# Attention probabilities transposed by VectorE and a trip through DRAM instead of by TensorE

## The chip, the cores and the metric

The kernel runs on one core of one Trainium2 chip. A time is the device time of one execution in microseconds (us), shorter being better. A comparison of two kernels is made between executions on the same chip.

## The reference

Pooled attention, and behind it a gated feed-forward block, in 32-bit floats:

```python
# q, k, v: [8 batches, 8 heads, 576, 64]
k_p = k.reshape(B, H, 72, 8, D).mean(axis=3)          # 576 keys pooled to 72
v_p = v.reshape(B, H, 72, 8, D).mean(axis=3)
scores = (1 / 8) * q @ k_p^T                           # [B, H, 576, 72]
attn = softmax(scores)                                 # 1e-9 added to the sum
x = (attn @ v_p) as [4608 tokens, 512]
out = ((x @ w1) * (x @ w2)) @ w3 @ w_out               # d_ff 1024, out [4608, 512]
```

## The kernel before

The 4608 tokens are worked in 12 chunks of 384. A chunk lies either in one batch (three tiles of 128 tokens) or across two (four tiles of 96): chunks 1, 4, 7 and 10 have four tiles, the others three. At the start w3 and w_out are multiplied into one matrix W, so that a chunk's feed-forward part is, for each of 8 blocks j of the inner dimension, a product a (12 matmuls, `a_mm`), a product b (12 matmuls, `b_mm`), their elementwise product g, and 9 matmuls of g with W (`out_mm`). The precision of a 32-bit product is kept by splitting each operand into a rounded high part and the remainder (hi and lo, or h and l in names) and doing three or four passes.

All work is written in one order by hand. A plan gives every piece of work a step; the pieces are sorted by step and, within a step, by kind: L (loads and stores on the DMA queue of SyncE, called SP), P (work of VectorE, ScalarE and GpSimd), M (feed-forward matmuls), A (attention matmuls). Each engine then runs its own pieces strictly in that order. A chunk m of the feed-forward part takes 24 steps: block j has its a at step 3j, its b at 3j+1 and its `out_mm` at 3j+5. The attention of chunk n stands in the same 24 steps as the feed-forward part of chunk n-1, which is called a period here. The attention of chunk 0 stands in the start, and that of chunk 1 in the period of chunk 0, where the weights w1 and w2 are still being split as well.

Attention of a chunk, for each token tile t: `s_mm` (scores, 8 matmuls in two halves), `soft1` and `soft2` (the softmax, in the tile E, 8 heads by 72 keys), `soft3` (the remainder keys copied to R), `pt_mm` and `ptr_mm` (transposes on TensorE into PSUM), `pt_post` and `ptr_post` (from PSUM into PTh, PTl and PTr). The 72 keys of a head are 64 main keys and 8 remainder keys. For a pair of heads 128 main keys make one 128-row transposed tile, four such for 8 heads; the 8x8 remainder keys, twice for the precision split, make two more. So a token tile has six transposes. When all tiles are through, `av_mm` (for each of four head pairs: PTh and PTl by the pooled values vbd, PTr by the remainder values VR) makes x for the chunk, and `av_post` splits it into the two tiles xT.

Other names: `qs` is the staging tile of q with one buffer, `qT` is q transposed by VectorE (`tr_q`), `st` the staging tiles of k and v with four buffers, POOL is GpSimd. The pool of PSUM for attention (`att`) has three buffers. `prep_vr` and `prep_vr2` pool and place the remainder values in VR.

The steps of the plan that matter, k being the first step of the period:

```python
s0, pt, av = (3, 5.5, 20.5) if n == 1 else (0, 6, 17) if nt == 4 else (0, 5, 15)
s_at = [k + s0 + 3 * t for t in range(nt)]
plan_att(n, s_at, 1, [x + pt for x in s_at], [k + av + pr for pr in range(NPR)])
plan_q(n, k - 18, 1, k - 9, 1)      # loads of q from step k-18, tr_q from step k-9
```

Of the kernel before, what the change touches and what calls it, by code (L numbers as in the profile page):

```python
# [18 lines left out]
def kernel(  # L19
# [52 lines left out]
    msk = cp.tile([P, 2], F32, name="msk")  # L72
# [182 lines left out]

    def load_q(n, prs=range(NPR)):
        if ("q", n) not in stage:
            stage["q", n] = p1.tile([P, NPR, CH // 32, 32], F32, tag="qs", name="qs")
        t = stage["q", n]
        for pr in prs:  # L260
            for (b, s0, cnt, off) in pieces(n):
                for par in range(2):
                    for db in range(2):
                        g = 2 * par + db
                        nc.sync.dma_start(
                            out=t[32 * g:32 * g + 32, pr, off // 32:(off + cnt) // 32],
                            in_=q[b, 2 * pr + par, s0:s0 + cnt, 32 * db:32 * db + 32].rearrange(
                                "(n t) e -> t n e", t=32),
                        )
# [3 lines left out]
    def tr_q(n, pr):  # L273
        if pr == 0:
            qT[n] = p1.tile([P, NPR, CH], F32, tag="qT", name="qT")
        nc.vector.transpose(
            out=qT[n][:, pr], in_=stage["q", n][:, pr].rearrange("p n e -> p (n e)"))
# [140 lines left out]

    def soft3(n, t):
        b, off, nt = tok_tiles(n)[t]  # L420
        E = Et[n, t]
        R = Rt[n, t] = p2.tile([P, NPR, 2, 2, 2, KR], F32R, tag="R", name="R")
        er = E[:nt].rearrange("p (a h) (x e) -> p a (h x) e", h=2, e=KR)[:, :, 0:18:17, :]
        for dup in range(2):
            nc.scalar.copy(out=R[:nt, :, :, dup, 0], in_=er)
        for dup in range(2):
            nc.vector.tensor_tensor(
                out=R[:nt, :, :, dup, 1], in0=er, in1=f(R[:nt, :, :, dup, 0]), op=ALU.subtract)
# [38 lines left out]
    def av_mm(n, pr):  # L467
        ps = patt.tile([P, 512], F32, tag="att", name="att")
        for (b, s0, cnt, off) in pieces(n):
# [3 lines left out]
            nc.tensor.matmul(out=o, lhsT=vh, rhs=PTh[n][:, pr, c], start=True, stop=False)  # L473
            nc.tensor.matmul(out=o, lhsT=vh, rhs=PTl[n][:, pr, c], start=False, stop=False)  # L474
            nc.tensor.matmul(out=o, lhsT=vl, rhs=PTh[n][:, pr, c], start=False, stop=False)  # L475
            nc.tensor.matmul(out=o, lhsT=VR[b % 2][:, pr], rhs=PTr[n][:, pr // 2, c], start=False, stop=True)  # L476
# [245 lines left out]
```

## Time and profile before

| What | us |
|---|---|
| median of 3 runs (lowest, highest) | 811.12 (809.81, 812.19) |
| span of the profiled execution, first to last instruction | 808.3 |
| PE (TensorE matmuls) busy | 776.7 |
| PEld (TensorE weight loads) busy | 722.8 |
| DVE (VectorE) busy | 431.2 |
| ACT (ScalarE) busy | 283.5 |
| POOL (GpSimd) busy | 193.8 |

The profile is of one execution, whose span is 2.8 us below the median of the runs. A row of the profile names the engine, the line of the kernel, the operation, what it wrote and read, and how often; then the busy time and the mean of one in nanoseconds, or in a timeline the start and the length. Matmuls are pipelined: one begins before the one ahead has ended, so what a matmul costs is the distance from its start to the start of the next, not its length. The granted TensorE clock was 0.985 of full speed on average.

### The profile page before, as it was taken

Reading aid. Unit: us, or ns where it says so; the run is one execution under the profiler, and the core shown is the slowest. Engines: PE = TensorE matmul, PEld = TensorE weight load, DVE = VectorE, ACT = ScalarE, POOL = GpSimd, SP = SyncE. Lnnn points to the kernel's source line nnn. Section 1 sums busy time; section 2 is a strip of 40 time slices with the busy share of each in tenths; the row PEclk is TensorE's granted clock in tenths of the full one; section 3 lists DMA queues with packets and bytes.
Section 4 is the critical chain, followed back from the end, with each engine's and each line's share of the span. In section 5 each row is a group of like instructions: output and inputs, shape, how many; then the busy total and the mean of one; then the engine's idle time right before and its main releaser. Section 6 shows DMA issues by size and latency. Waiting matters only on the chain.

```text
span 808.3 us, 11614 instructions
## 1 busy us (share of the span) xinstructions
PE 776.7 (96%) x4320; PEld 722.8 (89%) x4320; DVE 431.2 (53%) x881; ACT 283.5 (35%) x719; POOL 193.8 (24%) x234
## 2 busy tenths in 40 slices
PE   8879688899999999999999999999999999999998
PEld 7668677799999999999999999999999999999997
DVE  7858789556364465365374374374464465452112
ACT  5556555333233233242243233232233333232211
POOL 2244464207005403016008202034018021000000
PEclk9989899999999999999999999999999999999999
DMA  9997882036024230053034030071043110100101
GB/s 325 258 203 177 254 176 41 0 70 146 1 62 91 65 79 1 1 117 99 1 81 115 20 80 1 1 165 51 29 91 97 49 31 1 40 1 1 40 0 40
DMA packets 113160, 62.63 MB, mean 77 GB/s; under 512 B 80208, under 2 KB 96848, under 8 KB 113104
## 3 DMA queue, kind: packets, MB, share of 16 engines
q1 hardware_dynamic: 113104, 61.89, 30.7%
q8 instruction: 34, 0.56, 0.3%
q14 instruction: 22, 0.18, 0.1%
HBM read 52.43 MB, written 9.44 MB: 77 GB/s over the span
## 4 chain that ended last, share of the span: by engine, by line
PE 86%; DMA 5%; DVE 4%; issue 1%; SPq 1%; ACT 1%; POOL 0%; DVEq 0%
PE a L499 24%; PE b L499 24%; PE o L534 24%; PE att L378 4%; DMA st<-in_k_dram 2%; PE o L560 2%; PE att L438 2%; PE att L475 1%; PE att L473 1%; PE att L474 1%; PE att L476 1%; DMA qs<-in_q_dram 1%; PE att L448 1%; DVE wb L148 1%; DMA raw<-in_moe_w_out_dram 1%
## 5 line engine op out<-in xcount | busy, mean ns | idle before, releaser
L499 PE MATMUL a<-xT,hl 128*128 128x384 f32 x1152 | 222.6, 342 | 0.0
L499 PE MATMUL b<-xT,hl 128*128 128x384 f32 x1152 | 220.2, 339 | 0.0
L499 PEld LDWEIGHTS a<-xT,hl 128*128 128x128 f32 x1152 | 205.1, 191 | 4.7
L499 PEld LDWEIGHTS b<-xT,hl 128*128 128x128 f32 x1152 | 198.7, 188 | 0.0
L534 PE MATMUL o<-Wc,gh 128*128 128x512 f32 x576 | 183.6, 400 | 0.0
L534 PEld LDWEIGHTS o<-Wc,gh 128*128 128x128 f32 x576 | 105.2, 189 | 17.3
L519 DVE TENSOR_TENSOR a<-b,a 128x384 f32<-128x384 f32 x96 | 53.1, 554 | 125.6 <-PE b L499 125.6
L336 POOL TENSOR_TENSOR st<-st 72x512 f32<-72x512 f32 (+1 forms) x53 | 71.8, 1354 | 178.2 <-DMA st<-in_k_dram 163.5
L534 PE MATMUL o<-Wc,gl 128*128 128x512 f32 x288 | 114.0, 396 | 0.0
L509 ACT COPY a<-a 128x384 f32<-128x384 f32 x96 | 46.0, 479 | 182.3 <-PE a L499 163.3
L520 ACT CAST gh<-a 128x384 fp32r<-128x384 f32 x96 | 49.2, 512 | 147.8 <-DVE a L519 147.8
L525 DVE TENSOR_TENSOR gl<-a,gh 128x384 fp32r<-128x384 f32 x96 | 63.2, 659 | 35.8 <-ACT gh L520 35.4
L349 POOL TENSOR_TENSOR vbd<-vm,vbd 64x256 fp32r<-64x256 f32 x16 | 13.5, 842 | 253.3 <-ACT vbd L348 250.1
L534 PEld LDWEIGHTS o<-Wc,gl 128*128 128x128 f32 x288 | 54.1, 188 | 12.5
L485 DVE TENSOR_TENSOR xT<-att,xT 128x384 fp32r<-128x384 f32 x48 | 26.6, 556 | 70.7 <-ACT xT L484 70.7
L378 PE MATMUL att<-kbd,qT 128*128 128x144 f32 (+1 forms) x320 | 52.9, 289 | 4.3 <-ACT E L404 4.3
L400 DVE TENSOR_REDUCE sm<-E 128x4 f32<-128x288 f32 (+1 forms) x70 | 31.6, 451 | 46.3 <-ACT E L399 46.3
L378 PEld LDWEIGHTS att<-kbd,qT 128*128 128x128 f32 (+1 forms) x320 | 46.9, 180 | 5.7 <-ACT E L404 4.8
L394 DVE TENSOR_REDUCE mx<-att 128x4 f32<-128x288 f32 (+1 forms) x80 | 35.9, 450 | 28.1 <-PE att L378 28.1
L399 ACT ACTIVATE E<-E 128x288 f32<-128x288 f32 (+1 forms) x70 | 31.2, 445 | 55.5 <-DVE E L396 55.5
L560 PE MATMUL o<-hl 128*128 128x512 f32 x144 | 40.7, 421 | 4.8 <-DVE hl L177 4.8
L337 POOL TENSOR_TENSOR st<-st 72x256 f32<-72x256 f32 (+1 forms) x53 | 41.6, 784 | 4.2
(84 smaller groups left out, 796.0 us busy)
## 6 DMA issues: line engine op xcount, KB each, us to landing
raw<-in_moe_w_dram SPq DMA_DIRECT2D x32, 512.0 KB
st<-in_k_dram SPq DMA_DIRECT2D x32, 288.0 KB
out_dram<-ob SPq DMA_DIRECT2D x35, 256.0 KB
st<-in_v_dram SPq DMA_DIRECT2D x32, 256.0 KB
qs<-in_q_dram SPq DMA_DIRECT2D x128, 48.0 KB
raw<-in_moe_w_out_dram SPq DMA_DIRECT2D x8, 512.0 KB
st<-in_v_dram SPq DMA_DIRECT2D x64, 64.0 KB
qs<-in_q_dram SPq DMA_DIRECT2D x128, 24.0 KB
```

The source lines that it names most:

```text
L336: nc.gpsimd.tensor_tensor(out=t[:, :, 0:4], in0=t[:, :, 0:4], in1=t[:, :, 4:8], op=ALU.add)
L337: nc.gpsimd.tensor_tensor(out=t[:, :, 0:2], in0=t[:, :, 0:2], in1=t[:, :, 2:4], op=ALU.add)
L378: nc.tensor.matmul(out=ps[:nt, 2 * KP * j:2 * KP * (j + 1)], lhsT=qT[n][:, pr, off:off + nt], rhs=kbd[b % 2][:, pr], start=True, stop=True,)
L394: nc.vector.tensor_reduce(out=mx[:nt, hs], in_=sv, axis=AX.X, op=ALU.min)
L400: nc.vector.reduce_sum(out=sm[:nt, hs], in_=E[:nt, hs], axis=AX.X)
L499: nc.tensor.matmul(out=o, lhsT=w12[j, w][sw][:, kt * P:(kt + 1) * P], rhs=x[sx][:, kt], start=(i == 0), stop=(i == 3 * NK - 1))
L509: nc.scalar.copy(out=a, in_=gt[m, j][:, :CH])
L519: nc.vector.tensor_tensor(out=g, in0=ps[:, :CH], in1=g, op=ALU.mult)
L520: nc.scalar.copy(out=gh, in_=g)
L525: nc.vector.tensor_tensor(out=gl, in0=g, in1=f(gh), op=ALU.subtract)
L534: nc.tensor.matmul(out=oacc[m][t], lhsT=(gh, gl)[sg][:, c], rhs=W[j][sw], start=(j == 0 and i == 0), stop=(j == NJ - 1 and i == 2))
L560: nc.tensor.matmul(out=wacc[h][it], lhsT=w3t[s][sa][:, it * P:(it + 1) * P], rhs=wo[j][sb], start=(j == 0 and i == 0), stop=(j == NJ - 1 a ...
```

## The change

For chunks 1 to 11 (`n >= NT`, NT = 1) the six TensorE transposes of a token tile go, and with them `soft3`, `pt_post` and `ptr_post`. Instead:

- `te_turn`: VectorE transposes 32x32 blocks of E in place of the main keys into a tile T (which shares its buffer with `qs`), and of the remainder keys into Tr (which shares its buffers with R).
- `te_out`: two stores write T and Tr to a DRAM tile D. A chunk of three tiles has one such stage, a chunk of four tiles two, each of two tiles.
- `te_in`: eight loads bring D back with the blocks moved to their partitions: four into PTl (32 partitions each), four into PTr, which is the same data four times over.
- `te_post`, `te_rest`: ScalarE rounds PTl into PTh and the upper half of PTr, VectorE subtracts to leave the remainders, now once for half a chunk (128x768) and not once for a tile.
- The tokens of a chunk stand in another order within it (`tr_q` writes q in that order).
- In all chunks the remainder rows are re-laid: `load_vr` loads 8 rows of each head once and not four times, `prep_vr` copies them on chip, `prep_vr2` masks 128 rows and no longer adds 32.
- The steps move: scores come 2.5 steps apart and not 3 in chunks of four tiles, `av_mm` starts at step 19 (four tiles), 16 (three tiles) and not at 17 and 15, q is loaded from step k-8 and turned from k-4.

```diff
+    def te_turn(n, t):
+        ...
+        main = E[:nt].rearrange("p (a h) k -> p a (h k)", h=2)[:, :, KR:KR + P]
+        nc.vector.transpose(out=T[:nt, i, :, :, x].rearrange("p k a e -> p a k e"), in_=main)
+        nc.vector.transpose(out=Tr[:nt, i, :, x], in_=rest_keys(E, nt))
+
+    def te_out(n, i):
+        ...
+        d = stage["D", n, i] = dp.tile([P, 18 * 96], F32, tag="D", name="D")[:r, :18 * w]
+        nc.sync.dma_start(out=d[:, :16 * w], in_=T[:r, i].rearrange("p k a x e -> p (k a x e)"))
+        nc.sync.dma_start(out=d[:, 16 * w:], in_=Tr[:r, i].rearrange("p r x e -> p (r x e)"))
+
+    def te_in(n, i):
+        ...
+        for k in range(4):
+            nc.sync.dma_start(
+                out=f(lo[32 * k:32 * k + 32]).rearrange("p g a c -> p g (a c)"),
+                in_=d[:, :, 4 * w * k:4 * w * (k + 1)])
+        for q in range(4):
+            nc.sync.dma_start(
+                out=f(rest[32 * q:32 * q + 32]).rearrange("p g a c -> p g (a c)"), in_=d[:, :, 16 * w:])
+
+    def te_rest(n):
+        r = PTr[n]
+        nc.scalar.copy(out=r[:64], in_=f(r[:64]))
+        nc.vector.tensor_tensor(out=r[64:], in0=f(r[64:]), in1=f(r[:64]), op=ALU.subtract)
+
+    def te_post(n, x):
+        hi, lo = (t[n][:, 2 * x:2 * x + 2] for t in (PTh, PTl))
+        nc.scalar.copy(out=hi, in_=f(lo))
+        nc.vector.tensor_tensor(out=lo, in0=f(lo), in1=f(hi), op=ALU.subtract)
...
     def prep_vr(b):
...
+        pool_tree(stage.pop(("vr", b))[r], m[r])
+        nc.scalar.copy(out=c[r], in_=m[r])
+        nc.scalar.copy(out=c[64:96], in_=m[r])
+        nc.gpsimd.tensor_tensor(out=m[r], in0=m[r], in1=f(c[r]), op=ALU.subtract)
+        nc.scalar.copy(out=c[32:64], in_=m[r])
+        nc.scalar.copy(out=c[96:128], in_=m[r])
...
             at("P", k + 2, soft2, n, t)
+            if n >= NT:
+                at("P", k + 3, te_turn, n, t)
+                np_, ng, nx = split_of(n)
+                if t % nx == nx - 1:
+                    at("L", k + 4, te_out, n, t // nx)
+                    at("L", k + 5, te_in, n, t // nx)
+                continue
...
         for pr in range(NPR):
+            if n >= NT:
+                if pr < 2:
+                    at("P", av_at[0] - 2, te_post, n, pr)
+                elif pr == 2:
+                    at("P", av_at[0] - 1, te_rest, n)
...
-        s0, pt, av = (3, 5.5, 20.5) if n == 1 else (0, 6, 17) if nt == 4 else (0, 5, 15)
-        s_at = [k + s0 + 3 * t for t in range(nt)]
+        s0, ds, pt, av = (3, 2.5, 5.5, 20.5) if n == 1 else (0, 2.5, 6, 19) if nt == 4 else (0, 3, 5, 16)
+        s_at = [k + s0 + ds * t for t in range(nt)]
...
-            plan_q(n, k - 18, 1, k - 9, 1)
+            plan_q(n, k - 8, 1, k - 4, 1)
```

In `plan_att` the k of the second half's step is one above the tile's own, so `te_turn` of a tile stands 4 steps behind its first scores, `te_out` 5 and `te_in` 6. `av_mm` reads the loaded tiles through views with the tokens of a group together.

What stands in a row on PE between the `out_mm` of block 0 and the a of block 2, in the period that carries chunk 2 (o_ is `out_mm`, att with ident the transposes), before:

```order
L534 MATMUL o_1835<-Wc,gh 128x512 x2
L534 MATMUL o_1835<-Wc,gl 128x512
L534 MATMUL o_1836<-Wc,gh 128x512 x2
L534 MATMUL o_1836<-Wc,gl 128x512
L438 MATMUL att<-ident,E 128x128 x4
L448 MATMUL att<-ident,R 128x128 x2
L499 MATMUL a<-xT_1629,hl 128x384
L499 MATMUL a<-xT_1630,hl 128x384
```

and with the change:

```order
L619 MATMUL o_1815<-Wc,gh 128x512 x2
L619 MATMUL o_1815<-Wc,gl 128x512
L619 MATMUL o_1816<-Wc,gh 128x512 x2
L619 MATMUL o_1816<-Wc,gl 128x512
L584 MATMUL a<-xT_1608,hl 128x384
L584 MATMUL a<-xT_1609,hl 128x384
```

The six transposes between `out_mm` and a are gone, and nothing stands in their place.

On SP, from one group of output stores to the next, in the period that carries chunk 2 (qs, st are the loads of q, k and v), before:

```order
L549 DMA out_dram<-ob 128x512 x3
L265 DMA qs<-in_q_dram 32x12x32 x12
L281 DMA st<-in_k_dram 72x2x512
L265 DMA qs<-in_q_dram 32x12x32 x4
L281 DMA st<-in_k_dram 72x2x512 x3
L317 DMA st<-in_v_dram 64x2x512 x4
L330 DMA st<-in_v_dram 32x1x512 x8
L549 DMA out_dram<-ob 128x512 x3
```

and with the change:

```order
L634 DMA out_dram<-ob 128x512 x3
L296 DMA st<-in_k_dram 72x2x512 x2
L496 DMA D<-T 128x1536
L497 DMA D<-Tr 128x192
L518 DMA PTl<-D 32x4x384 x4
L522 DMA PTr<-D 32x4x192 x4
L296 DMA st<-in_k_dram 72x2x512 x2
L272 DMA qs<-in_q_dram 32x12x32 x16
L332 DMA st<-in_v_dram 64x2x512 x4
L345 DMA st<-in_v_dram 8x512 x8
L634 DMA out_dram<-ob 128x512 x3
```

The store to D and its return stand between the loads of k, and the loads of q have moved behind them, past all four loads of k.

On ScalarE, from the middle of the same period to the first cast of x (a, gh are `a_post` and the rounding of g), before:

```order
L460 CAST PTh<-att 128x4x128
L465 CAST PTr<-att 128x2x128
L509 COPY a<-a 128x384
L520 CAST gh<-a 128x384
L509 COPY a<-a 128x384
L484 CAST xT_2098<-att 128x384
L520 CAST gh<-a 128x384
L484 CAST xT_2098<-att 128x384 x2
```

and with the change:

```order
L605 CAST gh<-a 128x384
L594 COPY a<-a 128x384
L605 CAST gh<-a 128x384
L532 CAST PTh<-PTl 128x768 x2
L527 CAST PTr<-PTr 64x768
L594 COPY a<-a 128x384
L605 CAST gh<-a 128x384
L569 CAST xT_2063<-att 128x384 x2
```

The casts that came with each token tile are gone, and three wide ones stand ahead of an `a_post`: these wait for the loads from D, and everything behind them on ScalarE waits with them.

More of the change, by code (lines that the diff above doesn't have):

```diff
@@ L76 @@
         out=msk,
-        in_=ident.rearrange("p (a two e) -> p two a e", two=2, e=2 * KR),
+        in_=ident.rearrange("p (q j e) -> p j q e", j=4, e=KR),
         axis=AX.XY,
@@ L254, in tok_tiles, with split_of, qs_tile @@
         return res
+    def split_of(n):
+        return (1, 4, 3) if len(pieces(n)) == 1 else (2, 3, 2)
+    def qs_tile(name):
+        return p1.tile([P, 2048], F32, tag="qs", name=name)
     def load_q(n, prs=range(NPR)):
         if ("q", n) not in stage:
-            stage["q", n] = p1.tile([P, NPR, CH // 32, 32], F32, tag="qs", name="qs")
+            stage["q", n] = qs_tile("qs")[:, :NPR * CH].rearrange("p (a n e) -> p a n e", a=NPR, e=32)
         t = stage["q", n]
@@ L421, in soft3 @@
         E = Et[n, t]
[L422 to L428, printed above, removed]
+        R = Rt[n, t] = p2.tile([P, 2, 4, 2, 2, KR], F32R, tag="R", name="R")
+        er = rest_keys(E, nt).rearrange("p (g a) h e -> p g a h e", g=2)
+        for q in range(2):
+            nc.scalar.copy(out=R[:nt, :, q], in_=er)
+        for q in range(2):
+            nc.vector.tensor_tensor(out=R[:nt, :, 2 + q], in0=er, in1=f(R[:nt, :, q]), op=ALU.subtract)
     Tp = {}
@@ L450, in ptr_mm, with pt_tiles @@
         Tp[n, t, "r"] = rv
+    def pt_tiles(n):
+        PTh[n] = p1.tile([P, NPR, CH], F32R, tag="PTh", name="PTh")
+        PTl[n] = p1.tile([P, NPR, CH], F32R, tag="PTl", name="PTl")
+        PTr[n] = p1.tile([P, 2, CH], F32R, tag="PTr", name="PTr")
+    def te_turn(n, t):
+        b, off, nt = tok_tiles(n)[t]
+        np_, ng, nx = split_of(n)
+        i, x = divmod(t, nx)
+        E = Et[n, t]
+        w = 32 * nx
+        if t == 0:
+            stage["T", n] = [
+                qs_tile("T")[:, :np_ * 16 * w].rearrange("p (i k a x e) -> p i k a x e", i=np_, k=4, a=NPR, e=32),
+                p2.tile([P, 256], F32, tag="R", name="Tr")[:, :np_ * 2 * w].rearrange(
+                    "p (i r x e) -> p i r x e", i=np_, r=2, e=32)]
+        T, Tr = stage["T", n]
+        main = E[:nt].rearrange("p (a h) k -> p a (h k)", h=2)[:, :, KR:KR + P]
+        nc.vector.transpose(out=T[:nt, i, :, :, x].rearrange("p k a e -> p a k e"), in_=main)
+        nc.vector.transpose(out=Tr[:nt, i, :, x], in_=rest_keys(E, nt))
@@ L454, in pt_post @@
         if t == 0:
-            PTh[n] = p1.tile([P, NPR, CH], F32R, tag="PTh", name="PTh")
-            PTl[n] = p1.tile([P, NPR, CH], F32R, tag="PTl", name="PTl")
-            PTr[n] = p1.tile([P, 2, CH], F32R, tag="PTr", name="PTr")
+            pt_tiles(n)
         pv = Tp.pop((n, t))
@@ L472, in av_mm @@
             o = ps[:, c]
[L473 to L476, printed above, removed]
+            if n < NT:
+                ph, pl, pq = PTh[n][:, pr, c], PTl[n][:, pr, c], PTr[n][:, pr // 2, c]
+            else:
+                ph, pl, pq = (t[:, :, x] for t, x in zip(pt_views(n, i), (pr, pr, pr // 2)))
+            nc.tensor.matmul(out=o, lhsT=vh, rhs=ph, start=True, stop=False)
+            nc.tensor.matmul(out=o, lhsT=vh, rhs=pl, start=False, stop=False)
+            nc.tensor.matmul(out=o, lhsT=vl, rhs=ph, start=False, stop=False)
+            nc.tensor.matmul(out=o, lhsT=VR[b % 2][:, pr], rhs=pq, start=False, stop=True)
         Tp[n, pr, "x"] = ps
```

64 lines of the change are left out of this document (43 added, 21 removed).

## The prediction

> **What bounds the kernel now.** I read the page first, then busy time by period, then TensorE's timeline.
>
> ```profile
> PE 776.7 (96%) x4320; PEld 722.8 (89%) x4320; DVE 431.2 (53%) x881; ACT 283.5 (35%) x719; POOL 193.8 (24%) x234
> PE 86%; DMA 5%; DVE 4%; issue 1%; SPq 1%; ACT 1%; POOL 0%; DVEq 0%
> ...
> 92.87:165.18 72.31, 62.34 (x349) 57.93 (x347) 56.21 (x92) 35.49 (x104) 31.66 (x27) 0.95 0.41 98
> 223.60:281.85 58.25, 58.25 (x327) 54.93 (x327) 28.77 (x61) 19.11 (x47) 21.16 (x27) 1.00 0.31 75
> 281.85:341.61 59.76, 59.76 (x354) 56.38 (x353) 31.47 (x73) 19.36 (x51) 6.63 (x9) 1.00 0.12 27
> ```
>
> The chain that ended last is 86% PE. The three lower rows are periods: length, then busy PE, PEld, DVE, ACT, POOL, then clock, DMA share and GB/s. In a period with three tiles (58.25 us) and in one with four (59.76) PE is busy from end to end at a clock of 1.00, and DVE for about half. There an instruction taken off PE is time won, if nothing comes late for it. The first period is different: 72.31 us, of which PE works 62.34.
>
> **The change part by part.** First, what leaves PE.
>
> ```profile
> 414.21 0.60 PE L438 MATMUL att<-ident,E 128*128 128x128 f32 x4
> 414.65 0.38 PE L448 MATMUL att<-ident,R 128*128 128x128 f32 x2
> 414.78 2.35 PE L499 MATMUL a<-xT,hl 128*128 128x384 f32 x12
> ...
> 298.32 0.49 PE L438 MATMUL att<-ident,E 96*128 96x96 f32 x4
> ...
> 298.82 0.66 PE L378 MATMUL att<-kbd,qT 128*96 128x144 f32 x4
> ...
> 313.84 0.49 PE L438 MATMUL att<-ident,E 96*128 96x96 f32 x4
> ...
> 314.28 2.33 PE L499 MATMUL b<-xT,hl 128*128 128x384 f32 x12
> ```
>
> From start to start, the six transposes of a 128-token tile cost 414.78 - 414.21 = 0.57 us, those of a 96-token tile 0.50 or 0.44, say 0.47. Three tiles are 1.71, four 1.88. Chunks 2 to 11 stand in bound periods: seven with three tiles, 12.0, and three with four, 5.6. Sum: 17.6 us off the path.
>
> Next, the cover in the three-tile period that the first three of these rows are from. What is done there, and when, before:
>
> ```profile
> 423.38 0.69 DVE L461 TENSOR_TENSOR PTl<-att,PTh 128x512 fp32r<-128x512 f32 x1 [0.61 <-ACT PTh L460]
> 424.42 0.94 DVE L416 TENSOR_TENSOR E<-E,sm 128x576 f32<-128x576 f32 x1
> 434.76 0.51 ACT L520 CAST gh<-a 128x384 fp32r<-128x384 f32 x1 [2.26 <-DVE a L519]
> 435.99 2.27 PE L499 MATMUL a<-xT,hl 128*128 128x384 f32 x12
> 438.10 0.34 PE L473 MATMUL att<-PTh,vbd 128*128 128x384 f32 x1
> 438.28 0.34 PE L474 MATMUL att<-PTl,vbd 128*128 128x384 f32 x1
> ...
> L276 DVE STREAM_TRANSPOSE qT<-qs 128x384 f32<-128x384 f32 x48 | 27.3, 568 | 4.3 <-DMA qs<-in_q_dram 4.3
> L461 DVE TENSOR_TENSOR PTl<-att,PTh 128x512 fp32r<-128x512 f32 x24 | 16.6, 690 | 10.6 <-ACT PTh L460 10.6
> L461 DVE TENSOR_TENSOR PTl<-att,PTh 128x384 fp32r<-128x384 f32 x16 | 8.8, 548 | 10.7 <-ACT PTh L460 10.7
> L427 DVE TENSOR_TENSOR R<-E,R 128x64 fp32r<-128x64 f32 x48 | 11.7, 285 | 12.4 <-ACT R L425 12.4
> L460 ACT CAST PTh<-att 128x512 fp32r<-128x512 f32 x24 | 14.0, 583 | 18.8 <-PE att L438 18.8
> L460 ACT CAST PTh<-att 128x384 fp32r<-128x384 f32 x16 | 7.7, 483 | 0.0
> ```
>
> `av_mm` keeps its matmuls; its operand now comes in runs of 96 or 64 tokens. No row shows such an operand. The nearest are these matmuls themselves, 0.18 us from start to start; I charge nothing, and the far end is that they double: 16 x 0.18 = 2.9 us a chunk, 32 in all.
>
> The last tile's scaling (L416) ends at 425.36. With one tile's transposes off PE ahead of it (0.57) and L461 with its wait gone (0.61 + 0.69), it ends near 423.5. `te_turn`: DVE costs (690 - 548)/128 = 1.11 ns a column, so 512 columns take 568 + 142 = 0.71 us and the 64 at most 0.29: done at 424.5. Per tile this adds 1.0 to DVE and drops 0.69 and 2 x 0.285, so DVE has less to do up to there than before.
>
> Then SP and the DMA queue. The nearest prices of a store and a load:
>
> ```profile
> 803.64 2.13 SPq L549 DMA_DIRECT2D out_dram<-ob  x4
> 804.00:804.50 0.50, 0.39 (x2) 0.00 (x0) 0.42 (x1) 0.08 (x1) 0.00 (x0) 1.00 0.06 25
> 804.50:805.00 0.50, 0.00 (x0) 0.00 (x0) 0.12 (x1) 0.29 (x1) 0.00 (x0) 1.00 0.98 381
> ...
> 364.20 4.56 SPq L317 DMA_DIRECT2D st<-in_v_dram  x4
> 366.00:368.00 2.00, 2.00 (x13) 2.00 (x12) 1.60 (x3) 0.82 (x3) 1.92 (x3) 1.00 0.98 206
> 350.84 6.25 SPq L265 DMA_DIRECT2D qs<-in_q_dram  x12
> ```
>
> Stores from 128 partitions, issued from 803.64 on, move data from about 804.45 (0.8 us later) at 381 GB/s. Loads into 64 partitions run at 206 GB/s with the DMA engines 0.98 busy. Loads of long rows into 32 partitions are not shown; 206 is the nearest row, and 381 the end on the other side. An issue takes 6.25/12 = 0.52 us. The two stores are 884 KB (128 x 1728 x 4 bytes): 424.5 + 0.8 + 2.3 = 427.6, say 427.7. The loads wait for that on SP, in order. Their data comes from 428.5; PTl (786 KB) has landed at 432.3, PTr (393 KB) at 434.2, and the eight issues (4.2 us) run beside. Queued behind this wait are two loads of k and the loads of q, 16 or 32 issues: the last leaves at 427.7 + 4.2 + 1.0 + 16.6 = 449.5. The last `tr_q` stands at step 23, seven steps of 2.35 us behind `av_mm`, at 455, so the later place of the q loads costs nothing; were they 5 us later, DVE would wait, and the first scores of the next period behind it.
>
> `te_post` stands behind the rounding of g for block 4, which ended at 435.27 and will end 1.71 earlier, at 433.56. So PTl has 1.2 us to spare. A cast of 768 columns takes 583 + 2 x 100 = 0.78 us on ACT, a subtraction 690 + 284 = 0.97 on DVE. DVE has two of these, a `g_lo` (384 columns, 0.55) and `te_rest`: 433.56 + 0.78 + 3 x 0.97 + 0.55 = 437.8. PE wants `av_mm` at 438.10 - 1.71 + 2.11 = 438.5, since a b product, as long as the a from 435.99 to 438.10, now stands ahead. Cover left: 0.7, with the landing's 1.2 some 1.9 us. I take a stall of 0. Once the cover is gone, each us of delay costs 7 us, and ScalarE's `a_post` behind the waiting cast is late next.
>
> [...]
>
> In a four-tile period the second stage carries 442 KB out and 590 KB back: 0.8 + 1.2 + 0.8 + 2.9 = 5.7 us, in the 4.5 steps (12.5 to 17) before `te_post`, about 10.8 us. Hidden.
>
> The remainder rows:
>
> ```profile
> L338 POOL TENSOR_TENSOR vrm<-st 128x128 f32<-128x128 f32 x8 | 4.0, 499 | 0.6
> ```
>
> GpSimd gets one more operation of at most this size per batch, ScalarE one more cast and one more wait for it; `load_vr` brings a quarter of the bytes. Priced at nothing, under GpSimd's idle 76%; without that cover, 0.5 us for each of 8 batches.
>
> The first period:
>
> ```profile
> 116.32 0.51 PE L448 MATMUL att<-ident,R 96*128 96x96 f32 x2 [3.87 <-ACT E L404]
> 147.40 0.55 PE L448 MATMUL att<-ident,R 96*128 96x96 f32 x2 [2.42 <-DVE R L427]
> ...
> 140.75 0.54 DVE L525 TENSOR_TENSOR gl<-a,gh 128x384 fp32r<-128x384 f32 x1
> 155.37 0.25 PE L473 MATMUL att<-PTh,vbd 128*128 128x192 f32 x1
> ...
> 92.87:150.00 57.13, 47.16 (x257) 43.53 (x256) 52.14 (x85) 32.16 (x97) 31.63 (x27) 0.95 0.52 124
> ```
>
> PE waits here at transposes, 6.3 us in these two rows alone, and the transposes leave. But DVE is busy 52.14 of 57.13 us, the weights being still split, so I expect the waits to move to the b product (DVE frees its PSUM tile) and to `av_mm`. On DVE up to the `g_lo` that ends at 141.3, three turns (3.0) and a scaling with its small ones (1.3) come in and 2.8 go out (three pairs of L427, two L461); then comes the last turn: 143.8. Stores 0.8 + 1.2, four loads of q that wait for the same buffer and stand ahead 2.1, first data 0.8, PTl's half of 393 KB 1.9: 150.6; casts and subtractions 0.78 + 3 x 0.97: 154.3, against 155.37. I take 1.1 us gained. The bounds: 10 gained (all of 72.31 - 62.34), and 1.8 lost, with the loads at half of 206 GB/s (1.9 more for PTl, 1.0 for PTr).
>
> Sum, on the profiled execution: 808.3 - 17.6 - 1.1 = 789.6. Its span is 2.8 under the median of the runs shown (811.12), so 792.4 there.
>
> **The rivals.**
> 1. *The round trip is late in the three-tile periods.* For: loads into 32 partitions are not shown, and the cover is 1.9 us. Against: nothing else is in the DMA queue then. Beyond the cover by 1 to 2 us, 7 to 14 us come back: 799 to 806. By 2.5 us, with PTl landing at 432.3 + 1.9 + 2.5 = 436.7 (12.2 us after `te_turn`; I say 7.8), it eats the whole 17.6; by 3.5 us, 817. This one ends slower.
> 2. *The first period loses its waits.* For: the wait rows name the transposes. Against: DVE's 52.14. It gives 792.4 - 8.9 = 783.5.
> 3. *Nothing is freed*, because the transposes only fill time in which PE would wait for a or b to be emptied. Against it speaks the last chunk, which has no attention beside it:
>
> ```profile
> 752.06 2.11 PE a L499 x12
> 758.34 2.11 PE a L499 x12
> ```
>
> The 6.28 us from one block's a to the next are three products of 2.1 us with no wait between. 811; a chance of 0.02.
>
> **How the numbers follow.** Forecast 0.60 (788 to 797), round trip late with a gain left or none 0.17, late and slower 0.10 (a doubled `av_mm` is in it), first period freed 0.11, nothing freed 0.02. Predicted: 792.4. The range of 785 to 804 leaves out the slower case, the latest of rival 1 and the lowest of rival 2, some 2 in 10. 0.3%, 2.4 us, is about what a measurement of this kernel can tell from no change. Faster: 0.60 + 0.11 + 0.14 = 0.85; within 0.3%: 0.03 + 0.02 = 0.05; slower: 0.10.
>
> **What would show it.** Right: periods of 56.5 us (three tiles) and 57.9 (four) with PE full, `av_mm` waiting for nobody, the wide cast waiting little for DMA, PTl landing 7 to 9 us behind the turn. Wrong: a wait of a us or more ahead of `av_mm` in three-tile periods, `tr_q` waiting for loads of q, a first period under 66 us, or `av_mm`'s matmuls further apart than 0.18.

## The result, and the profile after

The changed kernel takes 800.39 us (median of 4 runs, 799.19 to 801.36) against 811.22 before: a ratio of 0.9868, 95% interval 0.9849 to 0.9887. It is faster by 1.3%, inside the range, but 8.0 us above the 792.4 that were predicted: 10.8 us gained where 18.7 were forecast.

The page of the changed kernel, its line of busy time and the chain that ended last:

```profile
PE 760.8 (95%) x4098; PEld 703.5 (88%) x4098; DVE 453.5 (57%) x892; ACT 270.2 (34%) x612; POOL 208.3 (26%) x240
PE 60%; DVE 15%; POOL 6%; DMA 6%; ACT 5%; issue 5%; SPq 1%; POOLq 0%; ACTq 0%; DVEq 0%
```

PE works 15.9 us less than before (776.7), but its share of the chain fell from 86% to 60%: it now waits for others in places. Where, the busy time by period shows (length, then busy PE, PEld, DVE, ACT, POOL, clock, DMA share, GB/s). The rows are the first period, a four-tile period, and the two kinds that the three-tile periods have become: kind A prepares the attention of chunks 2, 5, 8 and 11, kind B that of chunks 3, 6 and 9.

```profile
92.66:168.53 75.87, 64.11 (x324) 59.35 (x323) 52.67 (x92) 34.13 (x92) 33.08 (x28) 0.90 0.45 109
455.80:514.52 58.72, 58.13 (x329) 54.30 (x328) 33.24 (x72) 18.07 (x39) 12.11 (x16) 1.00 0.25 63
514.52:570.86 56.34, 56.34 (x309) 53.14 (x308) 31.67 (x62) 16.46 (x33) 15.87 (x18) 1.00 0.45 108
570.86:628.51 57.65, 56.58 (x310) 53.07 (x308) 32.58 (x65) 18.25 (x39) 19.40 (x23) 1.00 0.41 100
```

Forecast were 56.5 for three tiles and 57.9 for four. Kind A (56.34) is a little better than that and has no wait in PE; only the period of chunk 2 takes 56.90, with a wait of 0.29. Kind B is 1.1 us too long, the four-tile period 0.8, and the first period, forecast to be 1.1 us shorter, grew by 3.56. On the two profiled executions that adds up to 8.7 us (808.3 to 799.6): 0.2 ahead of the first period, 3.56 lost in it, 12.05 gained behind it. That the medians stand 10.8 apart comes from the span of the execution profiled before, 2.8 us under its median where that of the one after is 0.8 under. As the steady periods repeat from execution to execution, the medians say that about 1.2 us, and not 3.4, were lost up to the end of the first period.

What PE waited for in the changed kernel, the rows that matter (total, times, longest):

```profile
PE a L584 <- ACT a L594: 6.5, 2, 4.6
PE att L561 <- POOL st L349: 3.2, 3, 1.1
PE att L561 <- DVE PTr L528: 2.8, 2, 2.5
PE o L619 <- ACT gh L605: 1.8, 3, 0.6
```

L584 is `a_mm`, and its wait lies in the first period, as does the 2.5 us at L561, `av_mm`'s matmul of the remainder keys. The three waits of 1.1 are one in each period of kind B, the three of 0.6 (L619, `out_mm`) one in each four-tile period. These four rows are the questions of the experiments.

**Kind B.** The row says that PE waits for GpSimd, but the timeline says otherwise. The splitting of the returned data in kind B, with the GpSimd work that starts beside it and the PE row that waited:

```profile
595.58 0.35 SPq L496 DMA_DIRECT2D D<-T  x1
598.90 1.74 SPq L518 DMA_DIRECT2D PTl<-D  x4
601.38 2.67 POOL L379 TENSOR_SCALAR VR<-vrh,msk 128x128 fp32r<-128x128 f32 x4 [0.74 <-ACT vrh L372]
604.74 1.58 ACT L532 CAST PTh<-PTl 128x768 fp32r<-128x768 f32 x2 [0.28 <-DMA PTl<-D]
605.62 2.46 DVE L533 TENSOR_TENSOR PTl<-PTl,PTh 128x768 fp32r<-128x768 f32 x2 [1.70 <-ACT PTh L532]
607.22 1.99 POOL L348 TENSOR_TENSOR st<-st 72x512 f32<-72x512 f32 x1
608.00 1.64 DVE L610 TENSOR_TENSOR gl<-a,gh 128x384 fp32r<-128x384 f32 x1
609.67 1.37 DVE L528 TENSOR_TENSOR PTr<-PTr 64x768 fp32r<-64x768 f32 x1
611.14 0.42 PE L561 MATMUL att<-PTr,VR 128*128 128x384 f32 x1 [1.07 <-POOL st L349]
...
549.13 1.83 DVE L533 TENSOR_TENSOR PTl<-PTl,PTh 128x768 fp32r<-128x768 f32 x2 [1.55 <-ACT PTh L532]
550.88 0.55 DVE L610 TENSOR_TENSOR gl<-a,gh 128x384 fp32r<-128x384 f32 x1
551.46 0.95 DVE L528 TENSOR_TENSOR PTr<-PTr 64x768 fp32r<-64x768 f32 x1
```

VR was complete at 604.05, seven us before; what ended at 611.04, 0.1 ahead of the matmul, is `te_rest`'s subtraction (L528). The wait is for several semaphores, and the one that the view names is not the one that ended last. The last three rows are the same DVE work in kind A, where GpSimd stands still: 1.83, 0.55 and 0.95 us. In kind B, beside GpSimd's sums of k, they take 2.46, 1.64 and 1.37: 2.14 us more, of which 1.07 reach PE. ScalarE's wide cast waited 0.28 us for the data here, and 0.41 and 0.58 in the two other periods of kind B, but that isn't what PE waits for: `te_rest` ended 40.19, 40.19 and 40.18 us into the three periods.

**The four-tile period.** ScalarE and PE there:

```profile
487.38 0.30 ACT L368 CAST vrh<-vrm 32x128 fp32r<-32x128 f32 x1 [3.92 <-POOL vrm L350]
489.25 0.51 ACT L605 CAST gh<-a 128x384 fp32r<-128x384 f32 x1
489.81 0.73 PE L619 MATMUL o<-Wc,gh 128*128 128x512 f32 x2 [0.58 <-ACT gh L605]
```

ScalarE stands 3.92 us at the first cast of the remainder rows, waiting for GpSimd's sum, and the rounding of g queues behind it.

**The first period.** The end of chunk 1's round trip, and the clock behind the wait:

```profile
147.26 1.88 SPq L272 DMA_DIRECT2D qs<-in_q_dram  x4
149.18 1.89 SPq L518 DMA_DIRECT2D PTl<-D  x4
155.96 0.53 PE L561 MATMUL att<-PTr,VR 128*128 128x192 f32 x1 [2.54 <-DVE PTr L528]
155.96:162.50 6.54, 6.54 (x25) 6.54 (x26) 3.09 (x6) 1.47 (x3) 0.00 (x0) 0.51 0.38 61
```

Four loads of q are issued ahead of the returning loads; `av_mm` waits 2.54 us; and for 6.5 us behind the wait the granted clock is 0.51, so that the product a behind it, 2.27 us at 146.67, takes 4.10.

### The profile page after: what moved, and what is told of

It is laid out like the page before. It is cut to its first block, busy times and chain, and to the rows that moved or that the text cites. A ratio compares the mean times of both kernels' runs of the same rounds, so it can differ in the third digit from the quotient of the medians.

```text
span 799.6 us, 11405 instructions
## 1 busy us (share of the span) xinstructions
PE 760.8 (95%) x4098; PEld 703.5 (88%) x4098; DVE 453.5 (57%) x892; ACT 270.2 (34%) x612; POOL 208.3 (26%) x240
## 4 chain that ended last, share of the span: by engine, by line
PE 60%; DVE 15%; POOL 6%; DMA 6%; ACT 5%; issue 5%; SPq 1%; POOLq 0%; ACTq 0%; DVEq 0%
PE o L619 17%; PE a L584 17%; PE b L584 17%; POOL st L348 2%; DMA raw<-in_moe_w_dram 2%; PE att L392 2%; PE o L645 2%; DVE E L410 2%; DVE mx L408 2%; ACT E L413 2%; DVE E L430 2%; PE att L561 1%; POOL st L349 1%; DVE gl L610 1%; DVE sm L414 1%
## 5 line engine op out<-in xcount | busy, mean ns | idle before, releaser
L584 PE MATMUL a<-xT,hl 128*128 128x384 f32 x1152 | 224.2, 344 | 6.5 <-ACT a L594 6.5
L584 PEld LDWEIGHTS a<-xT,hl 128*128 128x128 f32 x1152 | 208.8, 192 | 13.7 <-ACT a L594 7.6
L584 PE MATMUL b<-xT,hl 128*128 128x384 f32 x1152 | 219.7, 338 | 0.0
L584 PEld LDWEIGHTS b<-xT,hl 128*128 128x128 f32 x1152 | 199.6, 188 | 0.0
L619 PE MATMUL o<-Wc,gh 128*128 128x512 f32 x576 | 183.3, 399 | 1.8 <-ACT gh L605 1.8
L348 POOL TENSOR_TENSOR st<-st 72x512 f32<-72x512 f32 (+2 forms) x53 | 76.0, 1435 | 259.6 <-DMA st<-in_k_dram 197.5
L619 PEld LDWEIGHTS o<-Wc,gh 128*128 128x128 f32 x576 | 105.2, 189 | 19.8 <-ACT gh L605 2.7
L619 PE MATMUL o<-Wc,gl 128*128 128x512 f32 x288 | 114.3, 397 | 0.8 <-DVE gl L610 0.8
L619 PEld LDWEIGHTS o<-Wc,gl 128*128 128x128 f32 x288 | 54.1, 188 | 14.6 <-DVE gl L610 2.2
L349 POOL TENSOR_TENSOR st<-st 72x256 f32<-72x256 f32 (+2 forms) x53 | 41.9, 790 | 4.2
```

The costliest lines, as they stand in the source:

```text
L348: nc.gpsimd.tensor_tensor(out=t[:, :, 0:4], in0=t[:, :, 0:4], in1=t[:, :, 4:8], op=ALU.add)
L349: nc.gpsimd.tensor_tensor(out=t[:, :, 0:2], in0=t[:, :, 0:2], in1=t[:, :, 2:4], op=ALU.add)
L584: nc.tensor.matmul(out=o, lhsT=w12[j, w][sw][:, kt * P:(kt + 1) * P], rhs=x[sx][:, kt], start=(i == 0), stop=(i == 3 * NK - 1))
L619: nc.tensor.matmul(out=oacc[m][t], lhsT=(gh, gl)[sg][:, c], rhs=W[j][sw], start=(j == 0 and i == 0), stop=(j == NJ - 1 and i == 2))
```

## The experiments

The length of the periods in each kernel, from the starts of each period's first a (more than one value where they differ). A ratio is to runs of the kernel before made beside that kernel, whose medians were 811.2 to 812.2:

| kernel | time, ratio to before | first | kind A | kind B | four tiles |
|---|---|---|---|---|---|
| before | 811.2 | 72.31 | 58.25 | 58.25 | 59.75 |
| changed | 800.39, 0.9868 | 75.87 | 56.34 (56.90 once) | 57.65 | 58.72 |
| 1 chunk 1 by TensorE | 800.8, 0.9862 (0.9839-0.9884) | 75.05 | 56.33 | 57.66 | 58.73 |
| 2 k sums early | 806.39, 0.9924 (0.9897-0.995) | 74.09 | 56.34 (57.66 once) | 59.3-60.9 | 58.74 |
| 3 remainder rows alone | 809.63, 0.9969 (0.9952-0.9986) | 69.94 | 58.25 | 58.26 | 59.95 |
| 4 q behind the return | 795.71, 0.9795 (0.9768-0.9823) | 70.50 | 56.34 | 57.65 | 58.75 |
| 5 chunk 1 undone wholly | 794.39, 0.9785 (0.975-0.982) | 69.45 | 56.34 | 57.63 | 58.74 |
| 6 remainder casts late | 797.03, 0.9818 (0.9785-0.9851) | 72.15 | 56.34 (56.63 once) | 57.12 | 57.75 |
| 7 `av_mm` a step earlier | 821.73 (one run) | 72.13 | 57.9-63.0 | 59.5-61.0 | 58.73 |
| 8 three mends | 791.03, 0.9757 (0.972-0.9793) | 71.01 | 56.34 (57.42 once) | 57.2-58.4 | 57.74 |
| 9 cover step, chunk 1 back | 786.61, 0.968 (0.966-0.97) | 69.25 | 56.28 | 56.34 | 57.74 |
| 10 cover step, q late | 789.76, 0.9711 (0.9691-0.973) | 70.44 | 56.30 | 56.32 | 57.74 |

The steady periods repeat to 0.05 us from kernel to kernel where nothing was edited in them, so an edit's price there is read from one trace. The first period moves with the clock from execution to execution: in the changed kernel and in 2, 6 and 7 it is the same instruction for instruction, and it took 75.87, 74.09, 72.15 and 72.13 us. So a single first period says little unless others or the medians bear it out.

**1. Chunk 1 transposed by TensorE.**

```diff
-    NT = 1
+    NT = 2
```

> The changed kernel, but chunk 1 is transposed by TensorE as chunk 0 is (the remainder rows stay in their new layout). Theory A: the first period grew by 3.6 us (72.3 to 75.9) because the turns and the trip through DRAM of chunk 1 come beside the splitting of the weights; taken out, the period returns to 72.3, give or take 0.7, and the time falls by 3.6 us to about 796.8. Rival: what the new remainder rows put on GpSimd and ScalarE, or the low clock alone, makes the period long; then it stays at 75 or more and the time at 800.4, or 802 with the transposes of chunk 1 back on TensorE.

The period stayed at 75.05 and the time at 800.8: theory A failed, as far as it blamed the turns and the trip alone. The rows of this kernel's PE in the first period show other waits, and the last row the clock there:

```profile
118.41 0.58 PE L464 MATMUL att<-ident,R 96*128 96x96 f32 x2 [3.83 <-ACT E L418]
126.81 1.27 PE L392 MATMUL att<-kbd,qT 128*96 128x144 f32 x4 [3.92 <-ACT E L418]
116.00:132.00 16.00, 9.67 (x36) 9.10 (x37) 11.22 (x21) 8.73 (x36) 8.10 (x7) 0.57 0.25 39
```

Both waits are for ScalarE's softmax, and in the 16 us around them the clock is 0.57. The diff has one more edit in this period that this kernel kept: the scores of chunk 1's tiles stand 2.5 steps apart and no longer 3.

**5. Chunk 1 undone wholly**, the same with the spacing of before:

```diff
-        s0, ds, pt, av = (3, 2.5, 5.5, 20.5) if n == 1 ...
+        s0, ds, pt, av = (3, 3, 5.5, 20.5) if n == 1 ...
```

> As the first experiment (chunk 1 transposed by TensorE), and chunk 1's score steps stand three steps apart again, as in the kernel before, and no longer 2.5. Theory B: in the first experiment the first period stayed at 75.05 us because the closer spacing puts more of chunk 1's softmax between the splitting of the weights on ScalarE and VectorE, and PE's waits of about 4 us for it bring the low clock; with three steps it falls to 70 to 72.5, and the time to 796 to 798. Rival: the new remainder rows, or the order of the other steps, make it long; then it stays at 74 to 76, and the time at 800.

The first period fell to 69.45 and the time to 794.39. The same stretch, with one long wait in place of two:

```profile
115.90 0.39 PE L464 MATMUL att<-ident,R 96*128 96x96 f32 x2 [3.86 <-ACT E L418]
116.00:132.00 16.00, 15.01 (x80) 13.96 (x81) 14.23 (x24) 12.01 (x45) 7.59 (x7) 0.89 0.15 25
```

So with TensorE's transposes the closer spacing cost 5.6 us of the period, and 6.4 between the medians; kernel 9, which has the same first period, repeats the length with 69.25. What the spacing costs with the trip through DRAM was not tried. That the first period can be as short as 69.45 with chunk 1 as before, while the one profiled before was 72.31, is the subject of the third experiment.

**4. The loads of q behind the return.**

```diff
-            plan_q(n, k - 8, 1, k - 4, 1)
+            plan_q(n, k - (7 if n == 2 else 8), 1, k - 4, 1)
```

> The changed kernel, but the loads of q for chunk 2 stand one step later, so that none of them is issued ahead of the loads that bring chunk 1's probabilities back (four are now, 1.9 us). Theory A: the return lands 1.9 us earlier, the 2.54 us wait of the first attention-times-value matmul in the first period shrinks to about 0.6, and as the idle time also costs a low clock for the 8 us behind it (some 2.8 us more), the period falls from 75.9 to about 71.2 and the time to about 796. Rival 1: idle time costs only itself: 1.9 us, 798.5. Rival 2: the place of these loads doesn't matter, for DVE or the landing of the remainder sets the end: 800.4.

Theory A held: the period fell by 5.4 us to 70.50 in the profiled executions and the median by 4.7 to 795.71. The same matmul, and the same window of time as above:

```profile
152.09 0.35 PE L561 MATMUL att<-PTr,VR 128*128 128x192 f32 x1 [0.27 <-DVE PTr L528]
155.96:162.50 6.54, 6.54 (x42) 6.15 (x41) 3.19 (x7) 1.80 (x4) 0.00 (x0) 1.00 0.22 36
```

The wait shrank by 2.27 us; the other 3.1 are the clock, which is 1.00 now where it was 0.51. The loss is not the same each time: in kernels 2, 6 and 7 the same wait was 2.21, 0.68 and 1.01 us, the clock in the 6.5 us behind it 0.74, 1.00 and 1.00. With the loads behind the return (4, 8 and 10) the wait was 0.27 or none and the period 70.45 to 71.01. So four DMA issues of 0.47 us had cost 1 to 5 us, and the changed kernel's profiled execution is the far end. The length of a wait doesn't set the clock alone: in the changed kernel's first period a wait of 1.89 us left the clock alone (1.00 in the 6.5 us behind it, a product of 2.36 us) where one of 1.86 did not (0.61 in the 4.4 us behind it, a product of 3.71 us; in kernel 7, behind the same wait of 1.85, 2.36). What brings the low clock is not shown.

**2. The sums of k early**, in the periods of kind B:

```diff
+            if b % 2:
+                plan_k(b, k - 3, k - 20, k - 18, 0.9, 0.5)   # loads and sums 4 to 5 steps earlier
+            else:
                 plan_k(b, k - 3, k - 16, k - 13, 2)
```

> The changed kernel, but for batches 3, 5 and 7 the loads of k and GpSimd's sums of it stand 4 to 5 steps earlier, ahead of the preparation of the remainder rows instead of beside the splitting of the returned probabilities. The period in which this falls (57.65 us, three of them) waits 1.07 us at the remainder's matmul. Theory A: VectorE's subtractions there have both inputs in SBUF and are slowed by GpSimd (2.46, 1.64 and 1.37 us in place of 1.83, 0.55 and 0.95 in the period without GpSimd), so that they end 2.1 us late; with the sums out of the way the wait goes, 3 x 1.07 = 3.2 us, 797.2. Rival 1: the returned data lands late, and that alone makes the wait: no change, 800.4. Rival 2: PE waits for GpSimd's VR, as the row of the waits names GpSimd: its end moves from 604.0 to about 605.5, the wait grows to 2.5, and the time to about 804.

None of the three came out as written: 806.39, and kind B grew to 60.63 in the period shown here. But the rows tell the theories apart:

```profile
246.06 1.13 DVE L430 TENSOR_TENSOR E<-E,sm 128x576 f32<-128x576 f32 x1
...
254.34 0.30 ACT L368 CAST vrh<-vrm 32x128 fp32r<-32x128 f32 x1 [7.46 <-POOL vrm L350]
256.75 1.22 PE L619 MATMUL o<-Wc,gh 128*128 128x512 f32 x2 [2.51 <-ACT gh L605]
...
259.07 1.83 DVE L533 TENSOR_TENSOR PTl<-PTl,PTh 128x768 fp32r<-128x768 f32 x2 [1.31 <-DMA qs<-in_q_dram]
260.81 0.55 DVE L610 TENSOR_TENSOR gl<-a,gh 128x384 fp32r<-128x384 f32 x1
261.39 0.95 DVE L528 TENSOR_TENSOR PTr<-PTr 64x768 fp32r<-64x768 f32 x1
265.18 0.34 PE L561 MATMUL att<-PTr,VR 128*128 128x384 f32 x1
```

With GpSimd out of the way the three subtractions take 1.83, 0.55 and 0.95 us, to the hundredth what they take in kind A. So the slowing by GpSimd is real. That L561 waits for nothing proves less, since PE was late itself. But kinds A and B can be compared where the data came equally late: in kernels 1, 4 and 5 the wide cast of kind A, where it waited for the data, started up to 34.4 us into the period, and `te_rest` ended at 38.6 or sooner, ahead of PE; in kind B the cast started at 33.7 to 34.1 and `te_rest` ended at 40.2, behind PE. Late data (rival 1) doesn't explain that, and VR (rival 2) was long complete. The sums now slow the softmax instead (L430, 0.76 us alone, takes 1.13, and L427 ahead of it 1.26 in place of 0.16), and as GpSimd comes to the remainder rows later, ScalarE stands 7.46 us at their cast, gh behind it, and PE 2.51 behind that.

**6. ScalarE's casts of the remainder rows late.**

```diff
         at("P", prep_r, prep_vr, b)           # GpSimd's sum
-        at("P", prep_r + 1, prep_vr2, b)      # (the casts stood in prep_vr)
+        at("P", prep_r + late, prep_vr1, b)   # the casts; late = 3.2
+        at("P", prep_r + late + 1, prep_vr2, b)
```

> The changed kernel, but ScalarE's four casts of the remainder rows stand 3.2 steps behind GpSimd's sum, behind the rounding of g of that step, and no longer directly behind the sum. Theory A: in the four-tile period the output matmul waits 0.58 us for gh because ScalarE stands 3.9 us at the first cast, waiting for GpSimd's sum; with the casts late that wait goes, 58.72 falls to about 58.1 in three periods, 1.7 us in all, 798.7. In the third kind of period VR comes about 2 us later, still ahead of the matmul that wants it. Rival: gh is late because VectorE makes the product before it late; the wait stays, 800.4.

Held, and more: the four-tile period fell to 57.75 (0.58 of wait and 0.4 of PE's own time, 0.24 of it in the first three matmuls of `out_mm` behind the wait: from their start to that of the next three it was 0.93 us in the changed kernel and is 0.69 here), kind B to 57.12. The busy time of the four-tile period:

```profile
451.41:509.16 57.75, 57.75 (x329) 54.44 (x328) 33.39 (x72) 17.96 (x39) 12.21 (x16) 1.00 0.27 68
```

PE is full; in kind B it still waits 0.55 us for `te_rest`. There the splitting now stands beside GpSimd's masking of the remainder rows and not beside its sums, and VectorE all but keeps its time (1.92, 0.55 and 0.95 us); it is GpSimd that is slowed, 3.99 us for the four maskings in place of 2.67.

**3. The new remainder rows alone**: NT = 12 and the steps of before.

```diff
-    NT = 1
+    NT = NCH
-        s0, ds, pt, av = (3, 2.5, 5.5, 20.5) if n == 1 else (0, 2.5, 6, 19) if nt == 4 else (0, 3, 5, 16)
-        s_at = [k + s0 + ds * t for t in range(nt)]
+        s0, pt, av = (3, 5.5, 20.5) if n == 1 else (0, 6, 17) if nt == 4 else (0, 5, 15)
+        s_at = [k + s0 + 3 * t for t in range(nt)]
-            plan_q(n, k - 8, 1, k - 4, 1)
+            plan_q(n, k - 18, 1, k - 9, 1)
```

> All chunks are transposed by TensorE and all steps stand as in the kernel before; of the change only the new layout of the remainder rows is left (a quarter of the loaded bytes, one more GpSimd operation and one more cast a batch). Theory A: it costs nothing by itself, 811.2 give or take 0.8, since the rounding of g that it delays by about 0.7 us had 1.2 us to spare in the four-tile period. Rival: the longer chain between ScalarE and GpSimd already makes the output matmuls of the four-tile period wait, 0.6 us in each of three, and something in the first: 813 to 814.

The new layout costs nothing with three tiles (58.25) and 0.2 us with four, and the time is 2.3 us better than before's, not equal. In the two traces the first period is shorter by as much (69.94 against 72.31), and two of PE's waits in it, 0.68 and 2.42 us, are gone. The scaling of the softmax ran beside GpSimd's splitting of weights there (its two operations took 1.26 and 1.56 us); with the longer preparation of the remainder rows GpSimd comes to that splitting some 3 us later in the period, and the same operations take 0.16 and 0.76. That the length follows from this luck of the order is read from the traces, not tried by itself.

**7. `av_mm` one step earlier.**

```diff
-        ... (0, 2.5, 6, 19) if nt == 4 else (0, 3, 5, 16)
+        ... (0, 2.5, 6, 19) if nt == 4 else (0, 3, 5, 15)
```

> The changed kernel, but in three-tile periods the attention-times-value matmuls and the splitting of the returned probabilities stand one step (2.1 us) earlier. It measures the cover that the round trip has. In the second kind of period the last subtraction ends 1.15 us ahead of the matmul that wants it, in the third kind 1.07 us behind it. Theory A: the cover is these 1.15 us and the data lands 9 us behind the turn; one step earlier the wait is about 1.0 in four periods and 3.2 in three, 4 + 3 x 2.1 = 10 us, about 811, and more if ScalarE, standing at the wide cast, holds up the rounding of g behind it. Rival: the data lands early, VectorE's place in the order alone sets the end, which moves along with the step: no new wait, 800.

Theory A had the direction and undershot: 821.73 in one run, kind A 57.9 to 63.0 us. PE's main new wait in this kernel, and a period of kind A:

```profile
PE att L561 <- DVE PTr L528: 10.2, 5, 2.9
346.28:406.30 60.02, 58.17 (x309) 54.59 (x308) 31.16 (x62) 16.39 (x33) 16.40 (x18) 0.97 0.43 101
```

Four of the five waits lie in kind A, 2.3 us on average in place of 1.0 (the fifth is in the first period), since the product of g and its rounding now come between the subtractions and the casts; in the period shown the clock is 0.97. In kind B the wait is 2.2 where 3.2 was expected. In all seven periods ScalarE's wide cast waits 2.4 to 3.8 us for the data: here the return does come late. Together they grew by 24 us for a step of 2.1.

**8. Three mends together**: the edits of 2, 4 and 6.

> The changed kernel with three edits together: chunk 2's loads of q one step later, the sums of k early for batches 3, 5 and 7, and ScalarE's casts of the remainder rows 3.2 steps behind the sum. Theory A: the gains add up: 4.7 us (the first period at 70.5), 3 x 1.07 (the third kind at 56.5, since ScalarE no longer stands at the casts while GpSimd is late) and 3 x 0.58 (the four-tile kind at 58.1): 800.4 - 4.7 - 3.2 - 1.7 = 790.8. Rival: with the k sums early the remainder rows come late for the matmul itself (GpSimd ends near 259 where it is wanted at 262 in that period) or ScalarE still blocks: the third kind stays at 57.6 or more and the time at 794 or above.

791.03 agrees with the sum, but not for the reasons given: the four-tile period is right (57.74), kind B is not (57.2 to 58.4; the execution profiled, 798.56, was the slowest of six). A period of kind B:

```profile
421.64 0.35 SPq L501 DMA_DIRECT2D D<-T  x1
426.95 1.74 SPq L523 DMA_DIRECT2D PTl<-D  x4
436.92 0.42 PE L566 MATMUL att<-PTr,VR 128*128 128x384 f32 x1 [0.88 <-issue]
```

The turn comes 25.8 us into the period in place of 24.7, for the sums now slow the softmax ahead of it; and here the loads followed the store after 5.3 us in place of 3.3. In both places tried, the sums slow work of VectorE that PE comes to wait for, so the next remedy is cover.

**9 and 10. A step of cover.** `av_mm` of the three-tile periods one step later, the splitting where it was, and the late casts of 6; in 9 with the edits of 5, in 10 with that of 4.

```diff
-        ... (0, 2.5, 6, 19) if nt == 4 else (0, 3, 5, 16)
+        ... (0, 2.5, 6, 19) if nt == 4 else (0, 3, 5, 17)
-                    at("P", av_at[0] - 2, te_post, n, pr)
+                    at("P", av_at[0] - 2 - (len(tok_tiles(n)) == 3), te_post, n, pr)
-                    at("P", av_at[0] - 1, te_rest, n)
+                    at("P", av_at[0] - 1 - (len(tok_tiles(n)) == 3), te_rest, n)
```

> Chunk 1 transposed by TensorE with its scores three steps apart; ScalarE's casts of the remainder rows 3.2 steps late; and in three-tile periods the attention-times-value matmuls one step (2.1 us) later, while the splitting of the returned data stays where it was. The sums of k stay beside that splitting. Theory A: with 2.1 us more cover neither VectorE's slowing by GpSimd (about 2 us) nor a return that is up to 2 us late reaches PE: 56.3 in all three-tile periods, 57.7 in the four-tile ones, and the time is 794.4 - 3 x 1.3 - 3 x 1.0 = 787.5. Rival: the step is taken back at the period's end, where the last of these matmuls feed the next chunk's first product and share PSUM tiles with the scores: the periods stay at 57 or more and the time at 791 or above.

> The same two edits of the steady periods, but chunk 1 goes through DRAM as in the changed kernel, with chunk 2's loads of q one step later. Theory A: 795.7 - 3.9 - 3.0 = 788.8, with the first period at about 70.5; if it is as fast as the kernel with chunk 1 on TensorE or faster, the trip pays in the first period too. Rival: in the first period the closer scores (2.5 steps) leave PE waiting about 4.6 us for ScalarE's copy of a, with the low clock behind it, in most executions: the time is 790 or more and scatters.

Theory A held in both: 786.61 and 789.76 us. The periods of kernel 9, kind A, kind B and four tiles, and `te_rest` in that kind B:

```profile
332.11:388.39 56.28, 56.28 (x309) 53.09 (x308) 31.18 (x62) 16.39 (x33) 15.71 (x18) 1.00 0.45 108
388.39:444.73 56.34, 56.34 (x310) 53.02 (x309) 33.04 (x65) 17.97 (x39) 18.77 (x22) 1.00 0.39 98
444.73:502.47 57.74, 57.74 (x329) 54.43 (x328) 33.38 (x72) 17.95 (x39) 12.43 (x16) 1.00 0.30 74
427.28 1.93 DVE L533 TENSOR_TENSOR PTr<-PTr 64x768 fp32r<-64x768 f32 x1
```

PE is full in all three, although `te_rest` (L533 here) is slowed to 1.93 us: the slowing is still there and reaches nobody. Kernel 9 beats both: 25.6 us or 3.2% (3.0 to 3.4) under the kernel before. Kernel 9 is 3.1 us better than 10, so chunk 1 on TensorE, three steps apart, beats the trip at 2.5 steps; the trip at three steps was not tried. Of the 3.0 us between the two spans 1.2 lie in the first period and 1.7 ahead of it.

## Why the prediction was right or wrong

- **What leaves PE** (1.71 and 1.88 us a period, 17.6 in all): right, a little small. With nothing waiting (kernel 9) it is 58.25 - 56.3 = 1.95 and 59.75 - 57.74 = 2.01, so 7 x 1.95 + 3 x 2.01 = 19.7. In the changed kernel 12.05 arrived; kind B lost 3 x 1.3 of it (1.07 of wait and 0.24 of PE's own time, 56.58 against 56.34), the four-tile periods 3 x 1.0 (0.58 and 0.4, 58.13 against 57.74), and the period of chunk 2 0.6.
- **`av_mm`'s strided operand at nothing**: right. These two rows of the changed kernel start 0.18 us apart, as before:

```profile
553.03 0.34 PE L558 MATMUL att<-PTh,vbd 128*128 128x384 f32 x1
553.21 0.34 PE L559 MATMUL att<-PTl,vbd 128*128 128x384 f32 x1
```

- **A stall of 0 in three-tile periods**: right in kind A, wrong in kind B, to which the period that the sum was made for (chunk 6) belongs. The step that failed is "433.56 + 0.78 + 3 x 0.97 + 0.55 = 437.8". The single durations were right (0.95 measured for the subtraction, 0.79 for the cast), but the four operations on VectorE, 3.3 us alone, took 5.47 beside GpSimd. The row that would have said so is in the trace of before: a subtraction out of PSUM kept its 0.54 us beside GpSimd, while L153, with both inputs in SBUF, took 1.22 in place of 0.68. By taking the probabilities out of PSUM the change moved `te_post` from the one class to the other. An operation with one input was slowed there as well: L140, between the two, took 1.38 us in place of 0.42.

```profile
132.11 2.07 POOL L336 TENSOR_TENSOR st<-st 128x512 f32<-128x512 f32 x1
132.62 0.54 DVE L461 TENSOR_TENSOR PTl<-att,PTh 128x384 fp32r<-128x384 f32 x1
134.26 0.80 POOL L337 TENSOR_TENSOR st<-st 128x256 f32<-128x256 f32 x1
134.38 1.22 DVE L153 TENSOR_TENSOR hl<-wb,hl 128x512 fp32r<-128x512 f32 x1
```

- **The round trip**: the store side was right (loads issued 3.3 us after the store's issue, 3.2 said), the return slow: PTl landed 5.8 us after its first issue where 4.6 were summed, 9.2 after the turn and not 7.8. PTr's and k's loads are issued before PTl is in, and share the queue; that they are what made it slow was not tried. The cover of kind A took it, with 1.15 us to spare between `te_rest`'s end (552.41) and the matmul that wants it (553.56). Rival 1 was right in its place and wrong in its mechanism: late data is not what PE waits for in the changed kernel's kind B. It is in one place, the period of chunk 2, where the loads followed the store after 4.4 us, for 0.29 us. That the time, 800.39, falls into this rival's 799 to 806 is luck, and that it falls into the range owes as much to the width of the range as to the sum: the difference is made of three losses that neither the rival nor the sum names. The price of 7 us per us was too low: with `av_mm` earlier the seven periods grew by 24 us for 2.1.
- **The four-tile trip hidden**: right, ScalarE's wide cast waits for no DMA there.
- **Remainder rows at nothing, under GpSimd's idle 76%**: wrong cover. The cost is not GpSimd's time but ScalarE standing 3.9 us for it with gh queued behind. It stood 3.6 us before, too; by itself the new layout costs 0.2 us a four-tile period. With the transposes gone PE arrives earlier at `out_mm`, and the same wait becomes visible: 1.0 us a period.
- **The later place of q's loads**: right in the steady periods, where no `tr_q` waits for DMA; wrong in the first. The four loads ahead of the return were in the sum (2.1 us), but as an arrival of 154.3 against a PE that comes at 155.37. PE came at 153.4.
- **The first period, 1.1 gained**: wrong in sign. The profiled execution lost 3.56, beyond the bound of 1.8; the three others with the same first period lie between 1.8 lost and 0.2 gained, and the medians say about 1.2 lost. Two terms were missing: the closer spacing of chunk 1's scores, which was in the diff and got no price (what it costs is shown with TensorE's transposes alone), and the low clock behind a wait, which cost 3.1 us more behind the 2.54 of the profiled execution. Rival 2 (8.9 us gained, 783.5) is not borne out: the shortest first period here is 69.25, 3.1 gained, with chunk 1 on TensorE.

## What to carry to other kernels

Here the splitting, whose operand moved from PSUM to SBUF, took 5.47 us (with the subtraction of g in between) beside GpSimd's sums in place of 3.3, where a subtraction out of PSUM had kept its 0.54: before pricing an elementwise operation that will read two SBUF tiles, look for rows of that class beside GpSimd's work. Shortening the full engine made an old wait of its helpers visible, 1.0 us a four-tile period, so price every place where a helper already stands for another, not only what the change adds. And give a round trip through DRAM a step more of cover than its sum asks for: here one step of 2.1 us cost nothing and left PE full, which moving the sums to another place did not.

## What the runs showed of the hardware

- Behind a wait of 2.54 us on PE the clock was 0.51 for 6.5 us, behind the same wait at 2.21 us 0.74, at 1.01 and 0.68 us 1.00; of two waits of 1.9 us one brought the low clock (0.61 for 4.4 us) and one didn't (1.00).
- VectorE's subtraction of 768 columns with both inputs in SBUF takes 0.95 us alone and up to 2.08 beside GpSimd (in the first period). Beside GpSimd's sums VectorE was slowed (its four operations in kind B took 5.47 us in place of 3.3); beside its maskings GpSimd was (3.99 us for four in place of 2.67), and VectorE's took 3.42.
- From the issue of the 768 KB store to the issue of the loads that wait for it and the small store behind it, three-tile chunks took 3.3 to 4.0 us in 63 of 70 cases over ten traces, 4.4 in three and 5.2 to 5.7 in four. What makes the late ones is open.
